# Attention and token/channel mixer on one core: 29 of 168 squares of score tiles moved to GpSimd

## The chip, the cores and the metric

The kernel runs on one core of one Trainium2 chip. The metric is device time in microseconds of one execution. A core has five engines with an in-order queue each: TensorE (PE in the profile; its weight loads, which run beside the matmuls, are PEld), VectorE (DVE), ScalarE (ACT), GpSimd (POOL) and SyncE (SP). Here GpSimd issues the input loads, and SyncE the transposing DMAs and the stores. Engines wait for each other by semaphores. Matmul results stand in PSUM, in eight banks, until VectorE or ScalarE has read them.

## The reference

Two parts, one behind the other (8 batches, 12 heads, 448 tokens, head size 64):

```python
scores = scale * np.matmul(q, k.transpose(0, 1, 3, 2))
attn = np.maximum(scores, 0.0) ** 2 / S
x = np.matmul(attn, v)                       # heads side by side: (8, 448, 768)
h = np.maximum(x.transpose(0, 2, 1) @ w_tok1, 0.0) @ w_tok2
u = x + h.transpose(0, 2, 1)
out = u + np.maximum(u @ w_ch1, 0.0) @ w_ch2
```

The attention has no softmax: a score is cut at zero and squared. The square is what the change is about. The factors `scale**2 / S` are applied later, when the product with `v` leaves PSUM.

## The kernel before

**Steps and pieces.** A step `s` is one third of a batch, four heads; there are 24 steps, three to a batch. Each step's scores fall into 7 pieces `c` of 64 keys. A piece `S{s}.{c}` is four matmuls of TensorE into two PSUM banks (line 515). Two evictions `r{s}.{c}.0` and `.1` cut it at zero and bring it to SBUF as bf16, on ScalarE (line 343) or on VectorE (line 345). One square `q{s}.{c}` then squares both halves in place, as one 128 x 896 tile of bf16, on ScalarE (`AF.Square`, line 355) or on VectorE (a product of the tile with itself, line 357). `V{s}.{c}`, four matmuls (line 542), multiplies the squared piece with `v`; the seven `V` of a step add up in two PSUM banks. The squared tiles live in a ring of 12 buffers inside the SBUF tile `arena`, so a piece's eviction waits for the `V` of the piece 12 before it. There are 24 x 7 = 168 squares.

**What follows a step.** The result leaves PSUM (`xe`, lines 552 and 554), is transposed, goes through the token mixer (`t1`, `rt`, `t2`, `u`, lines 588 to 601), and once a batch's three steps are there, through the channel mixer. The first two batches use plain products (`C1`, line 623); the others one level of Strassen's scheme: `M1` (line 780) with evictions `s1` and `d1` (793, 796), and `M2` (line 847) with evictions `d2` (860, 862). Strassen's sums and differences of operands (`w`, `tu`, `h`) are VectorE instructions that read two SBUF tiles (line 688).

**Loads.** Each step's k, q and v come by six loads `ldk`, `ldq`, `ldv` of 112 KB (line 371) on GpSimd's queue. From step 10 on, k and q are rearranged in SBUF (`ik`, `iq`, line 351 on VectorE or 349 on ScalarE) and transposed by DMA (`xk`, `xq`, line 497, on SyncE).

**What sets the order.** One table of words, `ORDER`, written out by hand or by a planner, is read from front to back: each word emits one operation, and so fixes its place on its engine's queue. `:A` and `:D` behind a word choose ScalarE or VectorE. Digits behind a PE word name the PSUM banks it takes: `C1.1.2:7` fills bank 7, `c1e1.2:D` empties it on VectorE, and `S8.1:37` takes banks 3 and 7 again, so that it waits for that eviction. A name behind a load (`ldv9.0:xd6`) holds the load back until the named DMA is done.

Of the kernel before, what the change touches and what calls it, by code (L numbers as in the profile page):

```python
# [10 lines left out]
ALU = mybir.AluOpType  # L11
# [26 lines left out]
class Order:  # L38
# [55 lines left out]
wc2.1 r4.0.1:D q4.6:A S4.3:63 C1.0.10:0 cp5.1:D r4.3.1:A cp5.0:D q4.5:D r4.1.1:A X3.0:7 r4.0.0:A q4.1:A  # L94
xc3.0:D C1.0.1a:5 C1.0.1 q4.0:D ldv5.0 c1e0.10:A t1.3.0:3 r4.3.0:D c1e0.1:A wc2.2 q4.4:A q4.3:D ldk7.0 S5.3:24
S5.1:17 V4.0:06 r5.1.0:A V4.1 r5.3.1:D V4.2 V4.3 rt3.0:A r5.3.0:D V4.4 V4.5 r5.1.1:A V4.6 S5.0:54 S5.6:12
xe4.1:D xe4.0:A T6.0:37 r5.6.1:A r5.0.0:D S5.2:06 r5.2.0:D cp6.0:A X4.0:2 r5.6.0:D C1.0.5:5 cp6.1:A ldv5.1
xc4.0:D r5.0.1:A r5.2.1:A S6.0:03 r6.0.1:D S5.5:17 S6.1:24 q5.1:A C1.0.6:6 ldq7.1 r6.1.1:D ldv6.1 q5.6:A
r5.5.0:D C1.0.7:3 ldq10.0 c1e0.5:D c1e0.6:A r6.0.0:D r6.1.0:A r5.5.1:D S6.3:41 S6.4:56 S5.4:02 q5.3:D
C1.0.0a:7 r6.3.0:A q5.2:A r6.3.1:A C1.0.8:4 r5.4.0:A r6.4.0:A ldv7.1 q5.0:D r5.4.1:A t2.3.0:1 r6.4.1:A q5.4:A  # L100
c1e0.8:D C1.0.9:0 u3.0:D c1e0.9:A q6.3:D t2.3.1:5 C1.0.0 ldq9.1 C1.0.11:4 u3.1:D q6.4:A c1e0.0:D t1.4.0:2
# [6 lines left out]
d2.0.0.11b:D ldk10.1:ub0.0 r7.4.1:D ldk9.0:ub0.1 t2.4.1:5 h0.0.3:D M2.0.0.6 h0.0.2:D d2.0.0.22a:D T8.0:32  # L108
S7.2:61 d2.0.0.12a:D r7.2.0:A M2.0.0.3 ldq9.0:ub0.1 w1.0.0:D q7.4:A ldq11.1 u5.0:D q6.0:A t2.4.0:6 w2.2.0:D
# [9 lines left out]
q8.6:D r9.0.1:A r9.0.0:D w1.1.0:D c1e1.10:D r9.4.1:A C1.1.3:5 xq11 q9.0:D q8.4:D t1.6.0:6 q9.4:A q8.5:A
t1.7.0:3 ldq13.0:st1.0 rt6.0:A iq12:D ub1.2 c1e1.6:A ldk12.1:st1.64 ldq13.1:xd7 c1e1.3:D S9.2:27 rt7.0:A  # L120
S9.3:41 q8.1:D q8.3:D V8.0:56 r9.2.0:D r9.3.0:A V8.1 V8.2 r9.2.1:D S9.1:03 r9.3.1:A V8.3 S9.5:24 r9.1.0:A
r9.1.1:D V8.4 ldk14.0:xk11 S10.1:71 V8.5 r9.5.1:A V8.6 S9.6:03 r9.5.0:D xe8.0:D ldk12.0 ldk15.1 r9.6.0:A
q9.2:A t2.7.0:4 q9.5:D ldk13.0:st1.0 r9.6.1:A C1.1.11:2 q9.1:D ldq15.1 q9.3:A C1.1.7:5 t2.6.0:0 ldk13.1:xq11
# [15 lines left out]
r12.6.0:A V11.5 w1.3.0:D r13.0.0:A S12.5:53 V11.6 xe11.1:A t2.9.0:0 st4.64 r12.5.0:D M1.2.0.1:1 ldv12.0:ub2.2
r12.5.1:A ldq16.0:xk14 u9.0:D r13.0.1:A M1.2.0.5:7 tu2.1:D r12.6.1:A iq14:D S12.4:53 xe11.0:A S12.1:02 q12.3:D  # L140
xd11 w1.3.2:D s1.2.0.1:A M1.2.2.5:4 M1.2.2.1:6 r12.4.1:A r12.4.0:A M1.2.0.2:3 ldk17.1:st4.0 w1.2.1:D
s1.2.0.5:A q12.6:D w1.3.1:D M1.2.0.6 ldq17.0:ub2.1 q12.4:A d1.2.0.11:D tu2.3:D ldk16.0:ub2.1 r12.1.0:D
ldv13.1:xk14 s1.2.2.1:A t2.9.1:5 q12.0:A M1.2.0.3 M1.2.4.1:3 u9.1:D ub3.1 M1.2.2.2:0 r12.1.1:A s1.2.0.2:A
M1.2.2.6 d1.2.2.11:D s1.2.2.2:A xq14 M1.2.0.7 d1.2.0.12:D s1.2.2.5:A q12.5:A q12.2:D d1.2.0.22:D t1.10.0:5
M1.2.2.3 rt10.0:A q12.1:D d1.2.2.12:D xq15 M1.2.0.4 q13.0:A M1.2.2.7 y1.2.0:D S13.3:20 d1.2.2.22:D S13.1:75
r13.1.1:D V12.0:41 V12.1 V12.2 r13.3.1:A st6.64 st3.64 r13.3.0:A V12.3 V12.4 st5.0 r13.1.0:A V12.5 V12.6
q13.3:D S13.5:05 ub2.3 S13.4:27 xe12.1:A r13.5.0:D M1.2.2.4 s1.2.4.1:A xe12.0:D r13.5.1:A M1.2.4.2:1 r13.4.1:D
# [17 lines left out]
q15.5:D r15.6.0:A ldv17.1:xd13 q15.6:D M1.3.0.4 ldk20.0:xd13 c2e1.6.1:D S16.3:75 q16.0:A V15.0:41 r16.3.1:A  # L165
V15.1 ik19:D r16.3.0:D V15.2 V15.3 y1.3.0:A S16.5:06 r16.5.1:D V15.4 S17.1:35 st13.64 r16.5.0:A ub3.4 V15.5
S16.6:72 V15.6 r17.1.0:A q16.1:D q16.3:D S17.3:06 r17.1.1:A M1.3.2.1:3 r16.6.1:A xq18 ik18:D M1.3.2.5:5
xe15.1:A xe15.0:D s1.3.2.1:A M1.3.2.2:2 r17.3.0:D xd15 M1.3.2.6 r16.6.0:A r17.3.1:A d1.3.2.11:D s1.3.2.5:A
S16.2:14 S16.4:07 s1.3.2.2:A S17.4:62 r17.4.1:A r16.4.1:D M1.3.2.3 xk18 r16.4.0:A t2.13.0:7 d1.3.2.12:D
q17.1:A iq19:A xk19 M1.3.2.7 st13.0 r16.2.0:D t1.14.0:2 d1.3.2.22:D st6.0 q16.5:D M1.3.4.1:0 ub4.0 s1.3.4.1:A  # L170
r17.4.0:A r16.2.1:D M1.3.4.2:5 q17.3:A q16.2:D M1.3.4.5:1 xq19 rt14.0:A d1.3.4.11:D M1.3.4.6 t2.13.1:4 st12.64
M1.3.2.4 s1.3.4.2:A u13.0:D t1.15.0:6 s1.3.4.5:A q16.4:D u13.1:D q16.6:A M1.3.4.3 q17.4:D ub4.2 y1.3.2:A
M1.3.4.7 ldq23.1:st13.0 d1.3.4.12:D S17.0:57 ldk23.0:st13.0 ik20:D d1.3.4.22:D V16.0:24 V16.1 r17.0.1:A
S17.2:31 ldv19.1:st13.0 r17.0.0:D V16.2 ldq20.0 t2.14.1:7 rt15.0:A M1.3.4.4 ldv18.1 u14.1:D r17.2.1:A S17.6:65
V16.3 r17.2.0:A ldq22.0 y1.3.4:A q17.2:D S17.5:17 V16.4 r17.6.0:D r17.5.0:D V16.5 r17.5.1:A S18.3:30 V16.6
t2.14.0:6 xe16.0:A M2.1.0.2:7 h1.0.0:D M2.1.0.5:1 r18.3.0:A ldv20.0 q17.5:D q17.0:A h1.0.2:D ldk21.0:st13.64
r17.6.1:A ldk21.1 u14.0:D xe16.1:A S18.0:23 V17.0:56 d2.1.0.11a:D r18.0.0:A r18.3.1:D V17.1 V17.2 V17.3
# [826 lines left out]
```

## Time and profile before

| | |
|---|---|
| median of 3 runs (lowest, highest) | 345.86 us (342.97, 346.24) |
| profiled execution: time, span of its instructions | 344.49 us, 342.7 us |
| PE busy | 333.9 us, 97% of the span |
| DVE busy | 294.7 us, 86% |
| ACT busy | 250.1 us, 73% |
| POOL busy (issuing loads, nearly all of it) | 92.1 us, 27% |
| squares on ACT, line 355 | 76, 72.3 us |
| squares on DVE, line 357 | 92, 55.1 us |
| granted TensorE clock | 1.00 |

Times of single instructions come from the one profiled execution. The ends of matmuls are modelled in it, so a PE that is shown busy may still be waiting for a moment between two matmuls. DVE and ACT instructions that follow each other overlap a little in the records, and "busy" counts such a stretch once.

### The profile page before, as it was taken

The numbers are of one execution on the slowest core, as the hardware profiler recorded it, in microseconds if no ns is written. First come the engines' busy times: TensorE is split into PE (matmuls) and PEld (weight loads), VectorE is DVE, ScalarE is ACT, GpSimd is POOL, SyncE is SP. The second block draws the span as 40 slices with busy tenths as digits, with TensorE's granted clock in tenths as the row PEclk, the third lists the DMA queues.
The fourth block names the chain that finished last, engine by engine and source line by source line (L and its number), as shares of the span: only waits on it lengthen the run. The fifth ranks groups of instructions, "written<-read, shape, count | busy, mean of one in ns | idle before, by whom it ended". The sixth has DMA issues, their size and how long they took to land.

```text
span 342.7 us, 9412 instructions
## 1 busy us (share of the span) xinstructions
PE 333.9 (97%) x3797; PEld 222.5 (65%) x3797; DVE 294.7 (86%) x571; ACT 250.1 (73%) x462; POOL 92.1 (27%) x157
## 2 busy tenths in 40 slices
PE   7899999999999999999999999999999999999995
PEld 4456665655565658865578555876578777887753
DVE  2999998899899999998998999789986986838783
ACT  4999999858899789989799898979785832221000
POOL 8985422624251343131240712020020000000000
PEclk9999999999999999999999999999999999999999
DMA  8999999999999999999999997997676113432255
GB/s 151 178 183 192 205 209 186 133 141 158 177 191 172 176 142 155 223 174 144 167 201 191 157 143 153 151 162 132 135 148 87 25 31 80 89 79 62 71 147 153
DMA packets 98940, 50.20 MB, mean 146 GB/s; under 512 B 71568, under 2 KB 95952, under 8 KB 98896
## 3 DMA queue, kind: packets, MB, share of 16 engines
q1 hardware_dynamic: 72736, 26.92, 46.4%
q0 software_dynamic: 25136, 21.47, 45.3%
q10 hardware_dynamic: 1024, 1.21, 1.2%
q8 instruction: 29, 0.48, 0.6%
q14 instruction: 15, 0.12, 0.2%
HBM read 43.38 MB, written 11.01 MB: 159 GB/s over the span
## 4 chain that ended last, share of the span: by engine, by line
PE 85%; DMA 5%; ACT 4%; DVE 3%; issue 1%; SPq 0%; POOL 0%; ACTq 0%; DVEq 0%
PE m_ps L780 20%; PE m_ps L847 20%; PE sc_ps L515 9%; PE acc_ps L542 8%; PE m_ps L623 8%; PE t_ps L588 6%; PE h_ps L597 5%; PE m_ps L713 4%; ACT arena L343 3%; DMA arena<-in_q_dram 3%; DMA x_sb<-xT 2%; PE kqT_ps L472 1%; PE warm_ps L414 1%; PE x_ps L579 1%; DVE uT L601 1%
## 5 line engine op out<-in xcount | busy, mean ns | idle before, releaser
L343 ACT ACTIVATE arena<-sc_ps 128x448 bf16<-128x448 f32 x232 | 117.1, 593 | 16.8 <-PE sc_ps L515 16.2
L355 ACT ACTIVATE arena<-arena 128x896 bf16<-128x896 bf16 x76 | 72.3, 969 | 0.4
L345 DVE TENSOR_SCALAR arena<-sc_ps 128x448 bf16<-128x448 f32 x104 | 62.0, 616 | 3.7 <-PE sc_ps L515 3.3
L515 PE MATMUL sc_ps<-arena 64*64 64x448 bf16 x672 | 54.9, 357 | 2.2 <-ACT arena L349 1.2
L357 DVE TENSOR_TENSOR arena<-arena 128x896 bf16<-128x896 bf16 x92 | 55.1, 615 | 1.1 <-ACT arena L343 0.5
L371 POOL DMA_DIRECT2D arena<-in_q_dram x46 | 28.4, 619 | 80.9 <-DMA arena<-arena 29.2
L780 PEld LDWEIGHTS <-wc 128*128 128x128 bf16 x432 | 40.9, 98 | 5.1 <-issue 2.3
L371 POOL DMA_DIRECT2D arena<-in_v_dram x48 | 29.5, 619 | 54.4 <-DMA out_dram<-out_sb 21.9
L542 PE MATMUL acc_ps<-arena 64*64 64x448 bf16 x672 | 43.1, 350 | 0.2
L515 PEld LDWEIGHTS <-arena 64*64 64x64 bf16 x672 | 22.3, 105 | 24.1 <-issue 15.6
L371 POOL DMA_DIRECT2D arena<-in_k_dram x48 | 29.9, 633 | 25.2 <-DMA out_dram<-out_sb 10.0
L780 PEld LDWEIGHTS <-ws 128*128 128x128 bf16 x324 | 30.8, 98 | 3.9 <-issue 1.7
L847 PE MATMUL m_ps<-wc,r 128*128 128x384 bf16 x162 | 30.3, 327 | 0.0
L601 DVE TENSOR_TENSOR uT<-h_ps,xT 128x448 bf16<-128x448 f32 x48 | 29.1, 616 | 1.2 <-PE h_ps L597 0.9
L847 PEld LDWEIGHTS <-r 128*128 128x128 bf16 x216 | 20.4, 98 | 14.8 <-issue 2.6
L623 PE MATMUL m_ps<-uT,wc 128*128 128x448 bf16 x144 | 29.9, 353 | 0.0
L542 PEld LDWEIGHTS <-arena 64*64 64x64 bf16 x672 | 20.9, 106 | 11.3 <-issue 3.1
L793 ACT ACTIVATE arena<-m_ps 128x448 f32<-128x448 f32 x18 | 9.2, 542 | 23.7 <-PE m_ps L780 8.3
L780 PE MATMUL m_ps<-uT,wc 128*128 128x224 bf16 x216 | 25.3, 259 | 0.0
L588 PE MATMUL t_ps<-x_sb,wt 128*128 128x256 bf16 (+1 forms) x216 | 25.0, 261 | 0.1
L597 PE MATMUL h_ps<-wt,r_sb 128*128 128x448 bf16 x96 | 25.1, 353 | 0.0
L847 PEld LDWEIGHTS <-sums 128*128 128x128 bf16 x180 | 17.2, 98 | 12.0 <-issue 1.0
(86 smaller groups left out, 510.5 us busy)
## 6 DMA issues: line engine op xcount, KB each, us to landing
out_dram<-out_sb SPq DMA_DIRECT2D x42, 192.0 KB, 3.3
arena<-in_k_dram POOLq DMA_DIRECT2D x48, 112.0 KB, 5.0
arena<-in_v_dram POOLq DMA_DIRECT2D x48, 112.0 KB, 5.3
arena<-in_q_dram POOLq DMA_DIRECT2D x46, 112.0 KB, 4.9
wc<-in_moe_w_ch_dram POOLq DMA_DIRECT2D x6, 768.0 KB, 13.1
out_dram<-arena SPq DMA_DIRECT2D x4, 192.0 KB, 2.7
out_dram<-out_sb SPq DMA_DIRECT2D x8, 96.0 KB, 2.1
out_dram<-out_sb ACTq DMA_DIRECT2D x8, 96.0 KB, 2.4
```

The costliest lines, as they stand in the source:

```text
L343: nc.scalar.activation(out, ps, AF.Relu)
L345: nc.vector.tensor_scalar(out=out, in0=ps, scalar1=0.0, scalar2=None, op0=ALU.max)
L355: nc.scalar.activation(x, x, AF.Square)
L357: nc.vector.tensor_tensor(out=x, in0=x, in1=x, op=ALU.mult)
L371: o.ins = nc.gpsimd.dma_start(out=raws[t][s % NR][64 * half:64 * (half + 1)], in_=src[b, h0:h0 + 2].rearrange('e (p c) d -> p e (c d)', c=KC))
L515: nc.tensor.matmul(o.ps[e][64 * half:64 * (half + 1), :S], lhsT=lhsT, rhs=rhs, start=True, stop=True, skip_group_check=True)
L542: nc.tensor.matmul(o.ps[half][64 * e:64 * (e + 1), :S], lhsT=r[rows, e, c * D:(c + 1) * D], rhs=sq[rows, e, :], start=c == 0, stop=c == KC ...
L588: nc.tensor.matmul(o.ps[:, j, :], lhsT=wt1[:, c, j * 128:(j + 1) * 128], rhs=x_sb[:, p0:p1, c, :], start=c == 0, stop=c == 3)
L597: nc.tensor.matmul(o.ps[:, :S], lhsT=r1[:, j, a * 128:(a + 1) * 128], rhs=wt2[:, j, :], start=j == 0, stop=j == JC - 1)
L623: nc.tensor.matmul(ps[:, :S], lhsT=wc1[:, g, e * 128:(e + 1) * 128], rhs=uT[:, g, off:off + S], start=g == 0, stop=g == CC - 1)
L780: nc.tensor.matmul(o.ps[:, j * HB:(j + 1) * HB], lhsT=lhs[:, g, (e + j) * 128:(e + j + 1) * 128], rhs=rhs[:, g], start=j == g == 0 and not ...
L847: nc.tensor.matmul(o.ps[:, :HN], lhsT=lhs[:, e], rhs=rhs[:, e], start=e == 0 and not on, stop=e == EC // 2 - 1, skip_group_check=True)
```

## The change

A third letter, `:P`, sends an operation to GpSimd, and `square` learns to emit a product of the tile with itself there. In `ORDER`, 29 squares of steps 4 to 20 carry that letter: 16 that stood on ScalarE and 13 that stood on VectorE. Their words also stand at other places, mostly earlier, beside loads on the same queue. TensorE's words, SyncE's words and the loads stand in the order in which they stood, and so do all other words of ScalarE and VectorE among themselves. The code below line 356 moves down by two lines, so GpSimd's squares are line 357 of the changed kernel and VectorE's line 359.

```diff
-            if how in ('A', 'D'):
-                o.on = 'ACT' if how == 'A' else 'DVE'
+            if how in ('A', 'D', 'P'):
+                o.on = {'A': 'ACT', 'D': 'DVE', 'P': 'POOL'}[how]
...
-wc2.1 r4.0.1:D q4.6:A S4.3:63 C1.0.10:0 cp5.1:D r4.3.1:A cp5.0:D q4.5:D r4.1.1:A X3.0:7 r4.0.0:A q4.1:A
+wc2.1 r4.0.1:D q4.6:A S4.3:63 q4.4:P C1.0.10:0 cp5.1:D r4.3.1:A cp5.0:D q4.5:D r4.1.1:A X3.0:7 r4.0.0:A q4.1:A
...
     def square(o, x):
         if o.on == 'ACT':
             nc.scalar.activation(x, x, AF.Square)
+        elif o.on == 'POOL':
+            nc.gpsimd.tensor_tensor(out=x, in0=x, in1=x, op=ALU.mult)
         else:
             nc.vector.tensor_tensor(out=x, in0=x, in1=x, op=ALU.mult)
```

On GpSimd's queue, around steps 8 and 9, before: the DMA rows are loads, the last names what each waits for (DMASW and DMAHW are landings of DMAs).

```order
L371 DMA arena<-in_k_dram 64x2x448 [waits DMAHW0_49,DMASW4_49,DVE_49]
L371 DMA arena<-in_q_dram 64x2x448 [waits DMASW5_49]
L371 DMA arena<-in_v_dram 64x2x448 [waits DMAHW6_49,DMASW6_49]
L371 DMA arena<-in_v_dram 64x2x448 [waits DMAHW3_49,DMASW7_49,PE_49]
L371 DMA arena<-in_q_dram 64x2x448 [waits DMAHW3_49,DMASW0_49,PE_49]
```

The same place after, with the squares `q8.2`, `q8.6`, `q8.4` and `q9.0` as TENSOR_TENSOR rows; each waits for the two evictions of its piece.

```order
L373 DMA arena<-in_k_dram 64x2x448 [waits DMAHW0_49,DMASW4_49,DVE_49]
L373 DMA arena<-in_q_dram 64x2x448 [waits DMASW5_49]
L357 TENSOR_TENSOR arena<-arena 128x896 [waits PE_49,Activation_49]
L357 TENSOR_TENSOR arena<-arena 128x896 [waits DVE_49,PE_49,Activation_49]
L357 TENSOR_TENSOR arena<-arena 128x896 [waits Activation_49]
L373 DMA arena<-in_v_dram 64x2x448 [waits DMAHW6_49,DMASW6_49]
L373 DMA arena<-in_v_dram 64x2x448 [waits DMAHW3_49,DMASW7_49]
L357 TENSOR_TENSOR arena<-arena 128x896 [waits DVE_49,PE_49,Activation_49]
L373 DMA arena<-in_q_dram 64x2x448 [waits DMAHW3_49,DMASW0_49,PE_49]
```

Three squares now stand in front of the loads `ldv9.0` and `ldv10.1`, and one behind them.

On VectorE's queue at that place, before: the rows of L357 are squares (`q8.2`, `q8.6`, then `q9.0` and `q8.4` as one row x2), those of L688 are Strassen sums of weights (`w1.1.1`, `w1.1.0`), and the rest are evictions.

```order
L345 TENSOR_SCALAR r_75<-m_ps 128x448
L357 TENSOR_TENSOR arena<-arena 128x896
L688 TENSOR_TENSOR ws<-ws,wc_67 128x768
L345 TENSOR_SCALAR arena<-sc_ps 128x448
L357 TENSOR_TENSOR arena<-arena 128x896
L345 TENSOR_SCALAR arena<-sc_ps 128x448
L688 TENSOR_TENSOR ws<-ws,wc_67 128x768
L345 TENSOR_SCALAR r_75<-m_ps 128x448
L357 TENSOR_TENSOR arena<-arena 128x896 x2
```

And after:

```order
L345 TENSOR_SCALAR r_75<-m_ps 128x448
L690 TENSOR_TENSOR ws<-ws,wc_67 128x768
L345 TENSOR_SCALAR arena<-sc_ps 128x448 x2
L690 TENSOR_TENSOR ws<-ws,wc_67 128x768
L345 TENSOR_SCALAR r_75<-m_ps 128x448
```

Four squares have left VectorE there; evictions and sums keep their order.

Further on, on GpSimd's queue after, five squares stand nearly together (`q16.0`, then `q16.3`, `q17.1`, `q17.3`, `q16.2`), where before the loads followed each other:

```order
L373 DMA arena<-in_v_dram 64x2x448 [waits DMASW5_49]
L357 TENSOR_TENSOR arena<-arena 128x896 [waits DVE_49,Activation_49]
L373 DMA arena<-in_k_dram 64x2x448 [waits DMASW6_49]
L357 TENSOR_TENSOR arena<-arena 128x896 [waits DVE_49,Activation_49]
L357 TENSOR_TENSOR arena<-arena 128x896 [waits Activation_49]
L357 TENSOR_TENSOR arena<-arena 128x896 [waits DVE_49,Activation_49]
L357 TENSOR_TENSOR arena<-arena 128x896 [waits DVE_49]
L373 DMA arena<-in_q_dram 64x2x448 [waits DMAHW0_49,DMASW7_49,Activation_49]
```

The load of k for step 20 (`ldk20.0`) stands behind the first of the five, and `ldq23.1` behind the last.

More of the change, by code (lines that the diff above doesn't have):

```diff
@@ L119 @@
[L119 to L123, printed above, removed]
@@ L139 @@
[L139 to L143, printed above, removed]
@@ L144 @@
[L144 to L147, printed above, removed]
+w1.0.2:D r8.2.1:A q7.1:D q7.6:A xk10 S8.3:61 iq11:D q8.2:P S8.6:35 q7.5:D c1e1.1:D V7.0:04 V7.1 r8.3.1:A
@@ new lines @@
+ldv12.1:ub2.2 ik14:D t2.8.1:2 d2.0.5.22b:D ldk16.1:xk13 ldv13.0 S12.0:67 q11.5:A u8.1:D S12.2:40 rt9.0:A
+M2.0.5.3 tu2.2:D ub2.5 r12.2.1:A r12.2.0:D r12.0.0:A M2.0.5.4 r12.0.1:A q12.2:P xk14 q11.2:A q11.6:D S12.3:23
+S12.6:04 d2.0.5.21:D V11.0:67 V11.1 r12.3.0:A d2.0.5.12b:D V11.2 V11.3 xd10 r12.3.1:A iq15:D V11.4 S13.0:12
+tu2.0:D r12.6.0:A V11.5 q12.3:P w1.3.0:D r13.0.0:A S12.5:53 V11.6 xe11.1:A t2.9.0:0 st4.64 r12.5.0:D
+M1.2.0.1:1 ldv12.0:ub2.2 r12.5.1:A ldq16.0:xk14 u9.0:D r13.0.1:A M1.2.0.5:7 tu2.1:D r12.6.1:A iq14:D S12.4:53
@@ L164 @@
 t1.13.0:0 ldv18.0 d1.3.0.12:D q15.3:A C2.1.6.1:3 ldv17.0:xq16 d1.3.0.22:D r16.1.0:A r16.0.1:D rt13.0:A st11.64
[L165 to L177, printed above, removed]
-r18.0.1:A ldk22.0:ub4.0 q17.6:D S19.1:47 ldq21.0:xq19 S19.0:02 V17.4 V17.5 r19.1.0:D ldk22.1 V17.6 M2.1.0.1:3
```

208 lines of the change are left out of this document (115 added, 93 removed).

## The prediction

> **What bounds the kernel now.** I read the page first, then the stages, then TensorE's own waits. The page gives the busy time by engine and, at the end, the engines on the chain of waits that ended last.
>
> ```profile
> span 342.7 us, 9412 instructions
> PE 333.9 (97%) x3797; PEld 222.5 (65%) x3797; DVE 294.7 (86%) x571; ACT 250.1 (73%) x462; POOL 92.1 (27%) x157
> ...
> PE 85%; DMA 5%; ACT 4%; DVE 3%; issue 1%; SPq 0%; POOL 0%; ACTq 0%; DVEq 0%
> ```
>
> The changed squares stand between about 40 and 222 us, so I cut the span at 40 and 240. The columns are PE, PEld, DVE, ACT and POOL busy, then the granted clock, the DMA share and GB/s.
>
> ```profile
> 40.00:240.00 200.00, 199.12 (x2294) 128.36 (x2287) 184.84 (x357) 177.49 (x322) 59.40 (x100) 1.00 1.16 168
> 240.00:320.00 80.00, 79.57 (x740) 61.32 (x739) 61.41 (x118) 38.00 (x70) 2.36 (x4) 1.00 0.40 79
> 320.00:342.70 22.70, 18.51 (x130) 11.91 (x128) 14.99 (x31) 0.00 (x0) 0.00 (x0) 1.00 0.52 139
> ```
>
> TensorE is idle for 200 - 199.12 = 0.88 us in the stage of the change, and 0.43 us in the next. All its waits from 40 to 320 us are these:
>
> ```profile
> PE sc_ps L515 <- DVE uT L601: 0.5, 1, 0.5
> PE m_ps L780 <- ACT arena L793: 0.4, 1, 0.4
> PE sc_ps L515 <- DVE out_sb L722: 0.2, 1, 0.2
> ```
>
> So TensorE is the bound at full granted clock, and the whole gain that relief of other engines can give is 0.88 + 0.43 = 1.3 us; the idle 4.2 us at the end, after the last matmuls, belong to evictions and stores that the change does not touch. The other side is open. VectorE is busy 184.84 of 200 us beside it and ScalarE 177.49. How little room there is between an eviction and the matmul that takes the bank again shows in the order of time; the first row reads bank 7 (`c1e1.2`), the second fills it again (`S8.1`).
>
> ```profile
> 87.26 0.61 DVE L345 TENSOR_SCALAR r<-m_ps 128x448 bf16<-128x448 f32 x1
> ...
> 87.97 0.48 PE L515 MATMUL sc_ps<-arena 64*64 64x448 bf16 x4
> ```
>
> The eviction ends at 87.87, the matmul starts at 87.97: 0.1 us. There a VectorE that is 1 us late costs TensorE 0.9 us.
>
> **The change part by part.** What goes: 13 squares from VectorE and 16 from ScalarE, by these rows of the stage from 40 to 240 us.
>
> ```profile
> L357 DVE TENSOR_TENSOR arena<-arena 128x896 bf16<-128x896 bf16 x57 | 34.6, 616 | 1.0 <-ACT arena L343 0.5
> L355 ACT ACTIVATE arena<-arena 128x896 bf16<-128x896 bf16 x62 | 58.7, 966 | 0.3
> ```
>
> VectorE loses 13 x 0.616 = 8.0 us, ScalarE 16 x 0.966 = 15.5 us. Neither ends a wait of TensorE of any size, so by itself this is worth between 0 and -1.3 us; I take 0, because each of the three waits came once and ended with an eviction, none with a square.
>
> What comes: 29 squares on GpSimd. The trace has no such instruction. The nearest rows are GpSimd's own in the setup.
>
> ```profile
> masks.py:199 POOL TENSOR_SCALAR_AFFINE_SELECT ident<-ident 128x128 bf16<-128x128 bf16 x1 | 0.3, 288 | 0.1
> masks.py:197 POOL MEMSET ident<- 128x128 bf16 x1 | 0.2, 231 | 0.0
> L988 POOL MEMSET const-bfloat16-1.0<- 128x1 bf16 x1 | 0.1, 102 | 0.0
> ```
>
> One column costs 0.10 us, which is the fixed part. The select reads one operand and takes (0.288 - 0.10) / 128 = 1.47 ns a column more, so 896 columns with one operand would be 0.10 + 1.32 = 1.4 us. The square has two operands; read one after the other they would be 0.10 + 2.64 = 2.7 us. I take 2.1 us, halfway, and keep both ends. [...]
>
> The squares themselves can be hidden. GpSimd is busy 59.4 of the 200 us; 29 x 2.1 = 61 us more leaves it at 60%. What is queued behind a waiting or running square are loads. The tightest squares are the five around 175 to 187 us, of which `q16.2` is the last.
>
> ```profile
> 174.66 0.60 POOL L371 DMA_DIRECT2D arena<-in_v_dram  x1 [0.40 <-DMA arena<-in_k_dram]
> ...
> 175.30 0.72 POOL L371 DMA_DIRECT2D arena<-in_k_dram  x1
> ...
> 175.51 0.38 DVE L351 COPY arena<-arena 128x896 bf16<-128x896 bf16 x1
> ```
>
> ```profile
> 189.25 0.36 PE L542 MATMUL acc_ps<-arena 64*64 64x448 bf16 x4
> ```
>
> The first of the five can start at 175.3, behind `ldv17.0`; one load of 0.7 us stands between, so the fifth ends at 176.0 + 5 x 2.1 = 186.5, and `V16.2`, the matmuls that need it, start at 189.25: 2.7 us to spare. The cover is gone above (189.25 - 176.0) / 5 = 2.65 us a square. Of the loads, the closest is `ldv12.0`, which now waits for `q12.2` and `q12.3`.
>
> ```profile
> 126.38 1.24 POOL L371 DMA_DIRECT2D arena<-in_v_dram  x2
> ```
>
> ```profile
> 140.37 0.55 PE L542 MATMUL acc_ps<-arena 64*64 64x448 bf16 x8
> ```
>
> The row of these loads among the DMA issues of that stretch ends with the time to landing.
>
> ```profile
> arena<-in_v_dram POOLq DMA_DIRECT2D x2, 112.0 KB, 6.3
> ```
>
> It was the second of the two at 126.38 (about 127.0). Behind two squares it is issued at 127.0 + 4.2 = 131.2, lands 6.3 us later at 137.5, and `V12.0` needs it at 140.37: hidden, with 2.9 us left. So as long as nothing else is disturbed, the squares and loads cost 0.
>
> What may be disturbed is VectorE. A product of two SBUF operands on GpSimd runs beside VectorE's own: the squares that stay (57 - 13 = 44) and the Strassen sums of line 688, whose row in the same stage is
>
> ```profile
> 40.00:240.00 200.00, 34.13 (x63) 1.00 1.16 168
> ```
>
> That makes 44 + 63 = 107 VectorE instructions with two SBUF operands in 200 us, 0.535 per us. Nothing in the trace says what happens when one meets a GpSimd square, so I bound it. Least: both run at full speed, 0. Most: the two engines cannot read SBUF for two operands at once, and VectorE's instruction waits, with all behind it, until the square is done. For a square of 2.1 us the chance that one falls due is 1 - exp(-0.535 x 2.1) = 0.675, and the mean wait 2.1 - 0.675 / 0.535 = 0.84 us; 29 squares make 24.3 us (12.0 at 1.4 us a square, 36.9 at 2.7). The rows around 90 us show how thick they stand; first the last load in front of `q8.2` on GpSimd and the eviction of ScalarE for which `q8.4` waits, then VectorE.
>
> ```profile
> 85.97 0.62 POOL L371 DMA_DIRECT2D arena<-in_q_dram  x1
> ```
>
> ```profile
> 90.06 0.62 ACT L343 ACTIVATE arena<-sc_ps 128x448 bf16<-128x448 f32 x1
> ```
>
> ```profile
> 90.28 0.61 DVE L357 TENSOR_TENSOR arena<-arena 128x896 bf16<-128x896 bf16 x1
> 90.81 0.55 DVE L688 TENSOR_TENSOR ws<-ws,wc 128x768 bf16<-128x768 bf16 x1
> 91.64 0.62 DVE L345 TENSOR_SCALAR arena<-sc_ps 128x448 bf16<-128x448 f32 x1 [0.28 <-PE sc_ps L515]
> 92.19 0.62 DVE L357 TENSOR_TENSOR arena<-arena 128x896 bf16<-128x896 bf16 x1
> 92.72 0.62 DVE L345 TENSOR_SCALAR arena<-sc_ps 128x448 bf16<-128x448 f32 x1
> 93.25 0.55 DVE L688 TENSOR_TENSOR ws<-ws,wc 128x768 bf16<-128x768 bf16 x1
> ```
>
> With 2.1 us each, `q8.2`, `q8.6` and `q8.4` run one after another on GpSimd from 86.6 (85.97 + 0.62) to 92.9, the third from 90.8, just after its eviction is done (90.68). The sum of line 688 at 90.81 falls on the seam between two of them; the two evictions behind it (91.64, 92.72) free score banks that TensorE waits for. What of the 24.3 us reaches the end: 8.0 are paid by the squares that left VectorE; of its idle time, 200 - 184.84 = 15.2 us, between none and all can be used. That is 24.3 - 8.0 - 15.2 = 1 us at the least and 16 at the most. By the margin of 0.1 us above it is nearer to none, but a stall of TensorE also gives VectorE its lead back; I take half the idle time, 7.6: 24.3 - 8.0 - 7.6 = 8.7 us.
>
> Load issuing does not disturb VectorE in this way: the 57 squares on VectorE average 616 ns in the stage in which GpSimd issued about a hundred loads. A faint sign for a shared path is the load at 175.30, 0.72 us against 0.60 of the one before it, which ran over a VectorE copy between two SBUF tiles (175.51, above). [...]
>
> **The sum.** Against the profiled execution: 344.49 + 0 (relief) + 0 (squares and loads hidden) + 8.7 (VectorE held) = 353.2 us. That execution lies inside the runs of before (342.97 to 346.24, median 345.86), 1.8 us above its span.
>
> **The rivals.** (1) Nothing is held: the squares vanish behind TensorE. For it: TensorE idles 0.4% of the stage, and every cost above has cover. Against it: it needs 107 VectorE instructions to pass 29 squares freely. Time 344.5, from 343.2 (all idle of TensorE gone) to 346.5. It decides if the wait per square is below about (8.0 + 7.6) / 29 = 0.54 us. (2) GpSimd itself becomes late: a square over 2.65 us. At 3.5 us the five squares end at 193.5, 4.3 us behind `V16.2`, and `ldv12.0` lands at 127.0 + 7.0 + 6.3 = 140.3, just in time: 344.5 + 4.3 = 348.8. Against it: 3.5 lies above the upper end of 2.7. (3) Faster by over 1%: it would need 3.5 us where TensorE idles 1.3; only a change in how densely TensorE's matmuls follow each other, which the page models, could give it: 341 us. That the squares do not move at all is out: they stand on GpSimd's queue in the rows above.
>
> **How the numbers follow.** VectorE held 0.60, nothing held 0.33, GpSimd late 0.04, faster 0.03. The trace alone leaves the hold open between none and full; I lean to it because TensorE's slack lets through no gain and any hold beyond 0.54 us a square, out of a possible 0.84, costs time. The likeliest case by itself runs from 345.5 (24.3 us with all idle used) to 361 (none used, 16.3 more); with a square of 2.7 us it goes to 344.5 + 36.9 - 8.0 - 7.6 = 365.8, with 1.4 us to 344.5. About 1% is what a measurement of this kernel can tell from no change, that is 3.5 us. Of the 0.60, 0.55 are over it; with 0.04 of GpSimd late and 0.01 of the rest: slower 0.60. Same: 0.05 + 0.31 = 0.36. Faster 0.04. The range takes in nothing held and the full hold at 2.1 us, and leaves out some 0.05 below 343.5 and 0.12 above 361.
>
> **What would show it.** In the changed profile: the squares' row on GpSimd at 2.1 us (1.4 to 2.7); if they are held or hold, VectorE's rows for its own squares (line 359) and sums (line 690) rise above 616 and 550 ns, or gaps stand before them, VectorE's busy or waiting time in the stage goes up by some 16 us net though 13 squares left, and TensorE gets waits for VectorE's evictions of several us where it had 0.7. If those rows stay at their length and TensorE's waits stay near 1 us, the hold is wrong and the time is that of rival 1. Matmuls `V16.2` or `V12.0` waiting for GpSimd or a load would show rival 2. The prediction is wrong in its main step if a square takes 2 us and VectorE's two-operand rows are unchanged.

## The result

The changed kernel takes 358.24 us (median of 4 runs, 356.01 to 360.61) against 344.49 us before (median of 4, 342.97 to 346.24): a ratio of 1.0391, with a 95% interval of 1.0331 to 1.0451. It is 13.75 us slower. Its four executions fall into two pairs, 356.01 and 356.32 us at a mean granted clock of 1.00, 360.16 and 360.61 us at 0.993 and 0.995, and the profiled one is the longest, with a span of 357.3 us.

The page of the changed kernel, its span, the busy time by engine, and the engines on the chain that ended last:

```profile
span 357.3 us, 9449 instructions
PE 339.7 (95%) x3797; PEld 223.7 (63%) x3797; DVE 305.4 (85%) x558; ACT 237.8 (67%) x446; POOL 142.4 (40%) x186
...
PE 71%; DVE 12%; issue 5%; DMA 5%; POOL 3%; ACT 2%; DVEq 0%; ACTq 0%; POOLq 0%
```

VectorE has 13 instructions fewer and is busy 10.7 us longer (294.7 before); TensorE's share of the chain falls from 85 to 71% and VectorE's rises from 3 to 12%. The stages show where the time went. The stage of the change holds the same matmuls (2294 before, 2292 now) when it is cut at 254 us instead of 240; the columns are those of the prediction's rows.

```profile
40.00:254.00 214.00, 204.29 (x2292) 129.25 (x2291) 195.46 (x344) 165.05 (x306) 110.56 (x130) 0.99 1.05 157
254.00:334.00 80.00, 79.57 (x739) 61.20 (x737) 61.42 (x117) 38.58 (x71) 2.36 (x4) 1.00 0.41 79
334.00:357.30 23.30, 19.10 (x135) 12.39 (x132) 15.57 (x31) 0.00 (x0) 0.00 (x0) 1.00 0.51 136
```

Of the 14.6 us by which the span is longer, 14.0 lie in the first row: 214 us where it was 200. TensorE's idle time there is 214 - 204.29 = 9.71 us (0.88 before), and its busy time for the same matmuls is 5.2 us more; about 1.7 of these go with a lower clock (below), and the rest is not traced to a cause. The next stage is the same as before, the last 0.6 us longer. What TensorE waits for, of all that the kernel shows from 0.9 us up (who waits, for whom, us in total, times, longest):

```profile
PE sc_ps L517 <- DVE xT L556: 4.1, 2, 3.1
PE m_ps L849 <- DVE out_sb L864: 1.9, 3, 1.3
PE sc_ps L517 <- ACT arena L349: 1.2, 2, 0.7
PE warm_ps L416 <- DVE out_sb L413: 1.2, 1, 1.2
PE m_ps L849 <- DVE out_sb L862: 1.2, 1, 1.2
PE sc_ps L517 <- DVE out_sb L724: 0.9, 2, 0.7
PE sc_ps L517 <- DVE arena L345: 0.9, 3, 0.5
```

The first two and the fifth and seventh are evictions by VectorE that were not among the waits before, and the sixth has grown from 0.2; the other two were there with the same 1.2. The five make 9.0 us. None of the new ones is for a square, and for a load TensorE waits 0.2 us. So VectorE is late with its evictions. The groups of the stage from 40 to 254 us say why. First GpSimd's squares, from the page, then VectorE by form of instruction (count, busy us, mean ns of one):

```profile
L357 POOL TENSOR_TENSOR arena<-arena 128x896 bf16<-128x896 bf16 x29 | 49.8, 1721 | 43.3 <-ACT arena L343 21.4
```

```profile
L345 DVE TENSOR_SCALAR arena<-sc_ps 128x448 bf16<-128x448 f32 x79 | 47.0, 615 | 3.0 <-PE sc_ps L517 2.9
L359 DVE TENSOR_TENSOR arena<-arena 128x896 bf16<-128x896 bf16 x44 | 31.3, 717 | 0.6 <-ACT arena L343 0.2
...
L351 DVE COPY arena<-arena 128x896 bf16<-128x896 bf16 x19 | 12.4, 652 | 1.0 <-issue 1.0
...
L690 DVE TENSOR_TENSOR r<-r 128x768 bf16<-128x768 bf16 x7 | 5.3, 761 | 0.0
...
L690 DVE TENSOR_TENSOR ws<-wc,ws 128x768 bf16<-128x768 bf16 x3 | 3.1, 1040 | 0.0
```

The same forms before, from 40 to 240 us (the row of the squares, 616 ns, stands in the prediction):

```profile
L345 DVE TENSOR_SCALAR arena<-sc_ps 128x448 bf16<-128x448 f32 x79 | 47.2, 616 | 2.1 <-PE sc_ps L515 2.0
...
L351 DVE COPY arena<-arena 128x896 bf16<-128x896 bf16 x19 | 7.4, 387 | 1.7 <-DMA arena<-in_q_dram 1.5 <-issue 0.2
...
L688 DVE TENSOR_TENSOR r<-r 128x768 bf16<-128x768 bf16 x7 | 3.8, 549 | 0.0
...
L688 DVE TENSOR_TENSOR ws<-wc,ws 128x768 bf16<-128x768 bf16 x3 | 1.6, 549 | 0.0
```

The evictions, which read PSUM, are as long as before (615 ns against 616). The instructions that read and write only SBUF are longer: the squares 717 against 616, the sums up to 1040 against 549, and the copies, which the prediction had not counted, 652 against 387. Taken one by one (the duration of each VectorE instruction behind 30 us, less the median of its form before, counted where it is over 60 ns), 17 instructions are longer, 18.0 us in all. Five of them are copies, 5.1 us. The others all have two SBUF operands, and none reads PSUM. Where one ends behind a GpSimd square, it does so at a nearly constant distance: 0.48 us for a square of VectorE, 0.36 to 0.42 for a sum, 0.25 for a copy. That is the look of an instruction that is on record as started, stands until the square is done, and runs then.

The largest is a copy at 108.69 us: VectorE first, then GpSimd's queue, where `q10.1` and `q10.4` run one right behind the other.

```profile
107.09 0.61 DVE L603 TENSOR_TENSOR uT<-h_ps,xT 128x448 bf16<-128x448 f32 x1
108.69 3.06 DVE L351 COPY arena<-arena 128x896 bf16<-128x896 bf16 x1 [0.99 <-issue]
111.68 0.54 DVE L690 TENSOR_TENSOR sums<-r 128x768 bf16<-128x768 bf16 x1
112.15 0.61 DVE L556 TENSOR_SCALAR xT<-acc_ps 128x448 bf16<-128x448 f32 x1
```

```profile
107.56 0.59 POOL L373 DMA_DIRECT2D arena<-in_k_dram  x1 [0.61 <-PE sc_ps L517]
108.17 3.33 POOL L357 TENSOR_TENSOR arena<-arena 128x896 bf16<-128x896 bf16 x2
```

The copy (`ik12`) first comes 0.99 us late, because it waits for a load whose last packet lands at 108.62, and is then held for 2.68 us more than its 0.38; the pair of squares ends at 111.50, the copy 0.25 behind it. The eviction of line 556 stands in the queue two places further back, and it is the 3.1 us wait of TensorE in the table above. What followed was not in the prediction; in 2 us pieces, the granted clock is the third number from the end:

```profile
108.00:110.00 2.00, 1.71 (x15) 0.64 (x12) 1.30 (x1) 2.00 (x5) 1.99 (x3) 1.00 1.35 105
110.00:112.00 2.00, 0.00 (x0) 0.00 (x0) 2.00 (x2) 0.62 (x2) 1.50 (x1) 1.00 1.34 180
112.00:114.00 2.00, 1.19 (x8) 0.40 (x8) 2.00 (x5) 0.04 (x1) 0.00 (x0) 0.61 1.32 239
114.00:116.00 2.00, 2.00 (x8) 0.94 (x7) 1.82 (x4) 2.00 (x4) 0.64 (x1) 0.53 1.12 227
```

After standing for 3.1 us TensorE ran at 0.61 and 0.53 of its clock for 4 us, about 2 x 0.39 + 2 x 0.47 = 1.7 us more. The mean clock of 1.00 in 356.01 and 356.32 leaves no room for this fall; whether the stall was in them is not known, since only one execution was profiled.

### The profile page after: what moved, and what is told of

The parts are those of the page before. It is cut to its first block, busy times and chain, and to the rows that moved or that the text cites. A ratio compares the mean times of both kernels' runs of the same rounds, so it can differ in the third digit from the quotient of the medians.

```text
span 357.3 us, 9449 instructions
## 1 busy us (share of the span) xinstructions
PE 339.7 (95%) x3797; PEld 223.7 (63%) x3797; DVE 305.4 (85%) x558; ACT 237.8 (67%) x446; POOL 142.4 (40%) x186
## 4 chain that ended last, share of the span: by engine, by line
PE 71%; DVE 12%; issue 5%; DMA 5%; POOL 3%; ACT 2%; DVEq 0%; ACTq 0%; POOLq 0%
PE m_ps L849 19%; PE m_ps L782 18%; PE sc_ps L517 8%; PE m_ps L625 7%; PE acc_ps L544 7%; PE t_ps L590 5%; PE h_ps L599 4%; PE m_ps L715 3%; DMA arena<-in_q_dram 2%; POOL arena L373 2%; DMA arena<-arena 2%; DVE arena L359 2%; DVE arena L345 2%; DVE sums L690 2%; DVE out_sb L864 1%
## 5 line engine op out<-in xcount | busy, mean ns | idle before, releaser
L357 POOL TENSOR_TENSOR arena<-arena 128x896 bf16<-128x896 bf16 x29 | 49.8, 1721 | 43.3 <-ACT arena L343 21.4
L517 PE MATMUL sc_ps<-arena 64*64 64x448 bf16 x672 | 58.0, 360 | 7.8 <-DVE xT L556 4.1
L355 ACT ACTIVATE arena<-arena 128x896 bf16<-128x896 bf16 x60 | 57.3, 968 | 1.9 <-DVE arena L345 1.7
L359 DVE TENSOR_TENSOR arena<-arena 128x896 bf16<-128x896 bf16 x79 | 51.9, 672 | 0.7 <-ACT arena L343 0.2
L517 PEld LDWEIGHTS <-arena 64*64 64x64 bf16 x672 | 22.9, 105 | 32.9 <-issue 24.6
L849 PE MATMUL m_ps<-wc,r 128*128 128x384 bf16 x162 | 31.3, 334 | 0.0
L544 PEld LDWEIGHTS <-arena 64*64 64x64 bf16 x672 | 21.4, 106 | 11.1 <-issue 3.5
L798 DVE CUSTOM_DVE_ANT_0 r<-r,m_ps 128x448 bf16<-128x448 f32 x32 | 19.6, 615 | 6.6 <-PE m_ps L782 4.3
```

Of the source, the lines that this page charges most:

```text
L355: nc.scalar.activation(x, x, AF.Square)
L357: nc.gpsimd.tensor_tensor(out=x, in0=x, in1=x, op=ALU.mult)
L359: nc.vector.tensor_tensor(out=x, in0=x, in1=x, op=ALU.mult)
L517: nc.tensor.matmul(o.ps[e][64 * half:64 * (half + 1), :S], lhsT=lhsT, rhs=rhs, start=True, stop=True, skip_group_check=True)
L544: nc.tensor.matmul(o.ps[half][64 * e:64 * (e + 1), :S], lhsT=r[rows, e, c * D:(c + 1) * D], rhs=sq[rows, e, :], start=c == 0, stop=c == KC ...
L849: nc.tensor.matmul(o.ps[:, :HN], lhsT=lhs[:, e], rhs=rhs[:, e], start=e == 0 and not on, stop=e == EC // 2 - 1, skip_group_check=True)
```

## The experiments

The theory from these rows: a GpSimd instruction that reads SBUF holds VectorE's SBUF instructions, and with them the evictions behind them. The rivals: GpSimd's extra work costs in some other way (its queue, its loads, its semaphores); each square costs about the same wherever it stands; ScalarE and VectorE were worth more than TensorE's idle time showed. Each ratio below is against executions of the kernel before from the same session, whose medians run from 344.37 to 345.95 us; so the ratios compare better than the times.

**e1: the work of GpSimd alone.** All squares back on ScalarE and VectorE, and at the 29 places on GpSimd's queue two idle products on a tile that nothing else uses (the second waits for the first, since it reads what that wrote).

```diff
-            q4.4:P   (and 28 more)
+            g4.4     (and 28 more, squares as in the kernel before)
+                for _ in range(2):
+                    o.ins = nc.gpsimd.tensor_tensor(out=idle, in0=idle, in1=idle, op=ALU.mult)
```

> All 168 squares are back on ScalarE and VectorE as before; at the 29 places of GpSimd's queue stand instead two products each of an idle 128x448 tile with itself (about 1.7 us together), which wait for the same evictions as the square did and whose result nobody uses. Theory hold (a GpSimd product that reads SBUF keeps VectorE's two-operand instructions and SBUF copies waiting until it ends): VectorE's rows for squares and sums lengthen as in the changed kernel, and nothing is relieved, so as slow or slower than the changed kernel: 356 to 368 us. Theory queue (the squares cost because loads behind them on GpSimd come late): the same time as with idle writes instead of products, no longer VectorE rows. If what cost time was that a V matmul waited for a square on GpSimd: 344 to 346.

**e2: the same places, memsets.** Three idle memsets in place of the two products.

```diff
-                for _ in range(2):
-                    o.ins = nc.gpsimd.tensor_tensor(out=idle, in0=idle, in1=idle, op=ALU.mult)
+                for _ in range(3):
+                    o.ins = nc.gpsimd.memset(idle, 0.0)
```

> As the run with idle products, but three idle writes of a 128x448 tile (no operand read, about 1.7 us together) in place of each pair of products. Theory hold through the read path: two-operand rows of VectorE keep 616 and 550 ns; at most its copies between SBUF tiles are held; 344 to 348 us. If any GpSimd work beside VectorE holds it, or if the loads behind it are what is late: the same time as with the products.

e1 took 353.57 us, a ratio of 1.0261 (1.0203 to 1.0319); e2 344.79 us, 0.9995 (0.9961 to 1.0028). GpSimd's group of each:

```profile
L533 POOL TENSOR_TENSOR idle<-idle 128x448 bf16<-128x448 bf16 x58 | 60.2, 1037 | 42.0 <-ACT arena L344 23.5 <-DVE arena L346 12.8 <-DVE arena L352 2.8
```

```profile
L533 POOL MEMSET idle<- 128x448 bf16 x87 | 41.5, 477 | 41.3 <-ACT arena L344 25.2 <-DVE arena L346 12.4
```

So 60 us of products that nobody waits for cost 9 us, and 41 us of memsets in the same places cost nothing that can be measured. The products read SBUF and the memsets do not, and both stand in the same queue behind the same waits; so the queue and the waits are not the cause. (That the memsets are shorter is not it either: e8 below has 80 us in these places and loses 1%.) That it is the reads and not the arithmetic no run shows by itself; with one operand less to read the loss is smaller (e8). In e1 30 VectorE instructions are longer, 14.5 us in all, five of them copies; in e2 two copies, 0.4 us, each beside a memset. e1 lost less than expected, since none of its instructions is held for more than 0.77 us: VectorE gets its turn in the 0.08 us between two products. Here two of its squares and a copy pass, one behind each of the first three of four products in a row:

```profile
183.21 2.40 DVE L358 TENSOR_TENSOR arena<-arena 128x896 bf16<-128x896 bf16 x2
185.54 1.12 DVE L352 COPY arena<-arena 128x896 bf16<-128x896 bf16 x1
```

```profile
182.93 4.51 POOL L533 TENSOR_TENSOR idle<-idle 128x448 bf16<-128x448 bf16 x4 [0.37 <-DVE arena L346]
```

e2's profiled execution, 349.17 us, shows a late load and not a hold: `ik12` waits 2.49 us for it there (0.99 in the changed kernel, none in e1), and TensorE then stands for 1.99 us. So at this place a late load alone stalls TensorE, too.

**e3 and e4: the 29 squares in two parts.** e3 moves only the 12 squares that met no lengthened VectorE instruction in the changed kernel's trace, e4 only the other 17.

```diff
 e3: :P only on q4.4 q5.3 q5.6 q6.3 q8.2 q8.6 q8.4 q9.0 q12.1 q13.3 q17.3 q18.2
 e4: :P only on q7.4 q10.1 q10.4 q10.2 q11.1 q12.2 q12.3 q15.1 q15.2 q16.0 q16.3
                q17.1 q16.2 q19.1 q19.2 q19.4 q20.2
```

> Only the 12 squares during which no VectorE instruction was longer in the changed kernel's trace are on GpSimd (q4.4 q5.3 q5.6 q6.3 q8.2 q8.6 q8.4 q9.0 q12.1 q13.3 q17.3 q18.2); the other 17 are back where they were. Theory hold: the time of before, 343 to 347 us, as far as no new meeting comes up. If every square on GpSimd costs its share: 344.5 + 12/29 x 13.8 = 350 us.

> Only the other 17 squares are on GpSimd, those that overlapped a lengthened VectorE instruction. Theory hold: nearly the whole loss, 354 to 360 us. If every square costs its share: 344.5 + 17/29 x 13.8 = 352.6 us.

e3 took 346.24 us, 1.0047 (1.0015 to 1.0079), e4 354.45 us, 1.0287 (1.023 to 1.0344). Twelve squares cost 1.9 us and seventeen 10.1; by an even share it would have been 5.7 and 8.1. e3 speaks against the even share; e4 alone would not, with 2 us between its result and that share. In e4 17 instructions are longer, 15.5 us; in e3 two, 0.4 us. The two losses add up to 12.0 of the 13.75 us; the long hold of the copy by `q10.1` and `q10.4` in a row, and the clock after it, do not show in e4, although it has the pair as well. What the 1.9 us of e3 are is not settled: in its profiled execution (348.77 us, its longest) a load that landed late shows, and hardly a hold.

**e5: the pair taken apart.** `q10.1` and `q10.4` back on ScalarE, the other 27 as changed.

```diff
-q10.1:P ... q10.4:P
+q10.1:A ... q10.4:A
```

> The change with the two squares q10.1 and q10.4 given back to ScalarE, 27 squares left on GpSimd. In the changed kernel these two ran back to back, the copy ik12 on VectorE was recorded 3.06 us long behind them, and TensorE then stood for about 3 us and ran at a granted clock of 0.53 to 0.61 for the 4 us after. Hold (VectorE stands while a GpSimd square runs, and what counts is how long one instruction is held at a time): the stall of TensorE between 107 and 112 us is gone, the other sixteen held instructions stay; 350 to 354 us, so 4 to 8 us come back for 2 of 29 squares. Rival, every square costs about the same (13.75 us / 29 = 0.47 us each): 357.3 us. Rival, the clock drop and a late load make the stall, not the hold: 357 to 359 us and the stall at 107 to 112 us still there.

356.29 us, 1.0331 (1.0275 to 1.0386). The stall at 107 to 112 us is gone, as expected of the hold: the copy is short again, and no 2 us piece of the profile has a granted clock under 0.97.

```profile
107.91 0.39 DVE L351 COPY arena<-arena 128x896 bf16<-128x896 bf16 x1
```

But not 4 us came back; by the ratios it is 0.006 of 344.5, about 2, with intervals that overlap. The time by itself (354.0 to 357.8 us by its interval) fits the even share of 357.3 better than the 350 to 354 of the hold; it is the trace that speaks for the hold. Two reasons show for the small gain. 356.29 is what the two executions of the change at full clock took (356.01 and 356.32), so the costly stall may have been in the two others only. And the rest of the order met GpSimd elsewhere. Ten us later stands `q10.2`, which in the changed kernel held a sum for 0.99 us. Here it holds another one for 2.10 us, and that one was started 0.49 us ahead of it, while GpSimd still issued a load:

```profile
117.52 2.65 DVE L690 TENSOR_TENSOR sums<-sums,r 128x768 bf16<-128x768 bf16 x1
```

```profile
117.41 0.64 POOL L373 DMA_DIRECT2D arena<-in_q_dram  x1
118.01 1.74 POOL L357 TENSOR_TENSOR arena<-arena 128x896 bf16<-128x896 bf16 x1
```

So the size was a miss: which instruction meets a square is decided by a few tenths of a microsecond, and a stall taken out at one place can move the meetings behind it.

**e6 and e11: the squares in halves.** e6 makes each square two products of 448 columns; e11 puts a memset between the halves.

```diff
-            nc.gpsimd.tensor_tensor(out=x, in0=x, in1=x, op=ALU.mult)
+            for e in range(2):
+                nc.gpsimd.tensor_tensor(out=x[:, e], in0=x[:, e], in1=x[:, e], op=ALU.mult)
 e11, between the two:
+            nc.gpsimd.memset(idle, 0.0)
```

> Each of the 29 squares on GpSimd as two products of 128x448 with no wait between them, in place of one of 128x896. Hold lasting for one GpSimd instruction, and VectorE let in between two of them: a held instruction waits at most about 0.9 us in place of up to 1.7 us, its wait is about half as long, and the time falls to 348 to 353 us. If the next GpSimd instruction takes hold before VectorE gets in: as the change, 356 to 360 us. Rival, the cost is GpSimd's own time: the halves take a little longer together than one whole (two times the 0.89 us seen for bare 128x448 products against 1.68 us), so 358 to 361 us.

> The change with each of the 29 squares as two products of 128x448 and, unlike e6, an idle memset of 128x224 on GpSimd between them (the memsets of e2 hardly held VectorE). If it lets VectorE in between the halves: no VectorE instruction is held over two products (three were in e6, by 1.7 to 2.4 us), none longer than about 0.95 us, and 349 to 352 us. If it does not: as e6, 353 to 356 us. GpSimd's square is longer, about 2.2 us; one is due within 3.16 us of its operand (q16.2), so rival: where GpSimd comes late, TensorE waits for GpSimd at the V matmuls (L544) and 355 us or more.

e6 took 353.66 us, 1.0212 (1.013 to 1.0293), e11 355.75 us, 1.0293 (1.0205 to 1.0382). e6 lies just above its first expectation (inside it by the ratio, 351.8), e11 in the second of its own. The halves brought part of the loss back; with the memset less of it, if any. (A product of 128x448 takes 0.93 us by itself in e1 and e6, not the 0.89 of the expectation.) In e6 most holds end with one half, yet three last over more; in e11 one lasts over three halves and the memset between the first two:

```profile
86.75 3.90 DVE L361 TENSOR_TENSOR arena<-arena 128x896 bf16<-128x896 bf16 x1
```

```profile
86.58 0.62 POOL L375 DMA_DIRECT2D arena<-in_q_dram  x1
87.19 0.98 POOL L357 TENSOR_TENSOR arena<-arena 128x448 bf16<-128x448 bf16 x1
88.06 0.32 POOL L358 MEMSET idle<- 128x224 bf16 x1
88.31 0.97 POOL L359 TENSOR_TENSOR arena<-arena 128x448 bf16<-128x448 bf16 x1
89.19 0.96 POOL L357 TENSOR_TENSOR arena<-arena 128x448 bf16<-128x448 bf16 x1
90.07 0.31 POOL L358 MEMSET idle<- 128x224 bf16 x1
```

Each of these GpSimd records begins before the one ahead of it has ended (88.06 against 88.17), where in e1 0.08 us lie between. VectorE's square ended at 90.65, 0.50 us behind the third half, and TensorE waited for it at the V matmuls:

```profile
PE acc_ps L548 <- DVE arena L361: 2.3, 1, 2.3
```

That is a square of VectorE, not of GpSimd: the rival of a late GpSimd does not show, though a square took about 2.1 us there (the 3.16 us of the expectation are what `q16.2` had to spare behind its end in the changed kernel). So with a wait between two of GpSimd's products VectorE got in each time (longest hold 0.77 us in e1, and 0.63 in e10 below); where they follow at once, it gets in at some seams and not at others, memset or not. What decides it there is open.

**e7: the squares left out.** No engine computes the 29 squares.

```diff
+        if f'q{s}.{c}' in LEFT_OUT:
+            sq_ops[s, c] = ev
+            return u
```

> The 29 squares are left out altogether: they run on no engine, so ScalarE is rid of 16 and VectorE of 13 instructions and GpSimd has none. This gives the most that the relief could be worth. TensorE bounds the kernel and stands idle for 1.3 us between 40 and 320 us: 343 to 345 us, ratio 0.996 to 1.000. Rival, the two engines set a part of the pace by ways that the trace of before does not show as idle time of TensorE (a granted clock, say): 338 to 342 us, and then the holds cost that much more than the 13.75 us by which the change is slower.

343.97 us, 0.9987 (0.995 to 1.0025). Free removal of 23.5 us of work from the two engines is worth nothing that can be measured; TensorE is the bound, and with the rest of the order as it is, no other place for these squares can be expected to gain more.

**e9: relief and hold together.** The idle products of e1, and the 29 squares left out as in e7.

> The idle products of e1 at the same 29 places (two of 128x448 each), and the 29 squares left out altogether, as in e7. So GpSimd does what it did in e1, while VectorE is rid of 13 squares of 0.616 us (8.0 us) and ScalarE of 16 of 0.966 us (15.5 us). It tells whether relief of VectorE covers its holds, as the prediction's sum had it. e1 lost 9.2 us with 14.8 us held. If relief covers hold: 9.2 - 8.0 = 1.2 us are left, 345 to 347 us. If a hold costs where it strikes and relief elsewhere in the table gives nothing back: 351 to 354 us, as e1, with 25 or more VectorE instructions lengthened by 13 us or more.

350.95 us, 1.0131 (1.0066 to 1.0196), between the two expectations. Against e1 that is 0.013 of 344.5, 4.5 us (1.5 to 7.5 by the two intervals, which do not overlap). 25 instructions are longer, 11.7 us (14.5 in e1, by the count used here; the expectation has 14.8): part of what the relief gave is that fewer instructions stood there to be held. So 8.0 us taken from VectorE (with 15.5 from ScalarE) are worth roughly half of the 8.0 where holds set the pace, and zero where they don't (e7).

**e8 and e10: the kind and the length of GpSimd's instruction.** Both are e1 with another idle instruction.

```diff
 e8:
-                    nc.gpsimd.tensor_tensor(out=idle, in0=idle, in1=idle, op=ALU.mult)
+                    nc.gpsimd.tensor_scalar(out=idle, in0=idle, scalar1=0.0, scalar2=None, op0=ALU.max)
 e10, tensor_tensor on a tile of 224 columns:
-                for _ in range(2):
+                for _ in range(4):
```

> As e1 (all squares on ScalarE and VectorE, idle GpSimd work put beside them at the 29 places), but each idle product of two operands is replaced with an idle tensor_scalar maximum of one operand and the same 128x448 tile. If GpSimd holds VectorE only while it reads two operands from SBUF, as little as the memsets of e2: 344 to 346 us. If any read from SBUF holds it: as e1 in proportion to the time of one, 350 to 355 us with 15 or more VectorE instructions lengthened.

> As e1 (all squares on ScalarE and VectorE, idle products on GpSimd at the 29 places), but four products of 128x224 in place of two of 128x448, each again waiting for the one before. The sum of GpSimd's work is about the same (some 60 us) and the single hold is halved, to 0.45 us at most. If a queue in front of TensorE swallows some 0.2 to 0.3 us of each hold and only what is above it counts: 346 to 349 us. If the sum of the held time counts whatever its pieces (e1: 9.2 us for 14.8 held, 0.62): as many held us, more instructions, 351 to 354 us.

```profile
L533 POOL TENSOR_SCALAR idle<-idle 128x448 bf16<-128x448 bf16 x58 | 80.4, 1386 | 27.1 <-ACT arena L344 14.5
```

```profile
L533 POOL TENSOR_TENSOR idle<-idle 128x224 bf16<-128x224 bf16 x116 | 77.0, 664 | 26.8 <-ACT arena L344 12.7 <-DVE arena L346 3.9 <-DVE arena L352 2.5
```

e8 took 347.91 us, 1.0101 (1.0069 to 1.0133): with more time on GpSimd than e1, 22 instructions are longer by only 5.8 us, and most end while GpSimd's instruction still runs. Neither expectation was right: a one-operand read does disturb VectorE, but not until its end. e10 took 349.97 us, 1.0145 (1.0061 to 1.0229), again between its two: 34 instructions are longer, 10.3 us, the longest by 0.63 and not 0.45. The shorter pieces cut the sum of the holds (14.5 in e1); whether they also pass on a smaller share of it cannot be told, since the interval of e10 allows 2 to 8 us.

All of them side by side (held: VectorE instructions longer than before, counted as above in the profiled execution, which in e2, e3, e7 and e9 took 2.5 to 4.5 us more than the median):

| run | GpSimd work added, us | held | held, us | longest, us | time, us | ratio |
|---|---|---|---|---|---|---|
| the change | 49.9 | 17 | 18.0 | 2.68 | 358.24 | 1.0391 |
| e5 without the pair | 46.6 | 15 | 16.3 | 2.10 | 356.29 | 1.0331 |
| e11 halves, memset between | 65.9 | 26 | 17.0 | 3.28 | 355.75 | 1.0293 |
| e4 the 17 | 29.6 | 17 | 15.5 | 1.49 | 354.45 | 1.0287 |
| e1 idle products | 60.2 | 30 | 14.5 | 0.77 | 353.57 | 1.0261 |
| e6 halves | 58.4 | 21 | 17.3 | 2.42 | 353.66 | 1.0212 |
| e10 idle quarters | 77.0 | 34 | 10.3 | 0.63 | 349.97 | 1.0145 |
| e9 idle products, no squares | 57.4 | 25 | 11.7 | 0.77 | 350.95 | 1.0131 |
| e8 idle one-operand | 80.4 | 22 | 5.8 | 0.68 | 347.91 | 1.0101 |
| e3 the 12 | 20.5 | 2 | 0.4 | 0.35 | 346.24 | 1.0047 |
| e2 idle memsets | 41.5 | 2 | 0.4 | 0.26 | 344.79 | 0.9995 |
| e7 squares left out | 0 | 0 | 0 | 0 | 343.97 | 0.9987 |

The time does not follow GpSimd's work (29.6 us of it cost 2.9%, 80.4 cost 1.0%). It goes with the time that VectorE was held: in the runs with more than 5 us of it, the loss by the ratio is about 40 to 75% of the held time. The order is not strict (e6 has more held time than e4 and the smaller loss, though their intervals overlap), and the profiled execution need not be the typical one.

## Why the prediction was right, and where its sum was not

The direction, the mechanism and the place were right, and 358.24 lies in the range; the predicted 353.2 was 5.0 us too low, and that it came so near is in part luck. Step by step:

- **TensorE is the bound, relief is worth 0.** Right: e7 shows 0.9987 for the relief by itself.
- **A square on GpSimd takes 2.1 us.** Too long. It took 1.72 on the mean, from 1.67 to 2.05, inside the bounds of 1.4 and 2.7.
- **The squares and loads are hidden.** Right for the squares: by the records each was done at least 3.16 us (`q16.2`) before its V matmuls began, and no such wait appears. For loads it is not quite right: the copy at 108.69 waited 0.99 us for one, and that put it beside the pair of squares that held it.
- **VectorE is held for 24.3 us.** Held, yes; 18.0 us. With 1.72 us a square the prediction's own formula gives 1 - exp(-0.535 x 1.72) = 0.60 and a mean of 1.72 - 0.60 / 0.535 = 0.60 us, 17.3 us for 29 squares. The closeness is luck in part: the formula counts only instructions with two SBUF operands, and these were held for 18.0 - 5.1 = 12.9 us; the copies, which it leaves out, made up the rest. With the 19 copies counted in (126 in 200 us, 0.63 per us) it gives 0.67 us a square and 19.4 us. So its form was good, and the duration and the copies were the misses.
- **8.0 us of that are paid by the relief and 7.6 by half of VectorE's idle time.** This is the term that failed. Of 18.0 us only 18.0 - 13.75 = 4.3 were paid by the median, 18.0 - 14.6 = 3.4 by the span of the execution in which they were counted, not 15.6. e9 against e1 puts the relief at about 4.5 us instead of 8.0, which leaves nothing for the idle time in the change; yet e1, without relief, passes on 9 of its 14.5 us, so there is some cover where the holds are short. The prediction had the reason in hand: an eviction ended 0.1 us before TensorE needed its bank. The reading that fits is that a hold costs where it strikes, and that idle time of VectorE at other places of the stage does little against it; no run separates the two payments inside the change.
- **The sum.** The two wrong terms offset each other. With the true duration the prediction's sum would have been 344.5 + 17.3 - 15.6 = 346.2, and further off than it was.
- **Not foreseen:** the clock that falls after a stall of 3 us (1.7 us in the profiled execution), and two squares in a row (3.3 us) acting as one hold.

Of the signs that it named, TensorE's waits of several microseconds for VectorE, the longer rows of lines 359 and 690, and a busier VectorE all came, the last with 10.7 us (18.0 - 8.0 = 10.0) where 16 were named. Rival 1 (nothing held) falls with e1 beside e2. Rival 2 (GpSimd late) has no wait of TensorE for GpSimd in any of the traces. Rival 3 (faster) falls with e7.

## What to carry to other kernels

Before giving work to an idle engine, ask what else it shares with the busy ones: in these runs GpSimd products that read SBUF stopped VectorE's SBUF-to-SBUF instructions (17 of them for 18.0 us in the change and 30 for 14.5 us in e1, against two for 0.4 us beside the memsets of e2), and everything in VectorE's queue behind them (TensorE stood 3.1 us for the eviction at 112.15), even where no semaphore joins the two. Count such meetings near their full price (about 40 to 75% came through here) unless the place itself has slack, since idle time and relief elsewhere paid little for a wait in front of the bound engine (4.3 of 18.0 us in the change, by the median). And when the engine that bounds the kernel hardly idles (0.88 of 200 us here), first measure what leaving the work out altogether would bring (here nothing) before looking for a cheaper place for it.

## What the runs showed of the hardware

- **A hold looks like a long instruction, not like a gap.** The held instruction is on record as started, mostly with no idle time in front, and ends 0.25 to 0.5 us after the GpSimd product. Read the mean duration of a group against the kernel before.
- **GpSimd is held as well.** Of the 29 squares of the change, 21 took 1.67 to 1.70 us. The other eight, 1.71 to 2.05 us, all began while a VectorE instruction between SBUF tiles was running (of the 21, two did, in its last 0.04 us, and the second square of the pair at 108.17 began while the copy stood); the longest, at 188.83, began while a square of VectorE that the one before it had held ran until 189.34.
- **The hold can begin before the product.** In e5 and e11 VectorE instructions that were started 0.4 to 0.5 us ahead of a product, while GpSimd was still issuing a load, did not get done until products had ended (117.52 and 86.75 above). In the changed kernel a copy at 87.31, with the issue of two loads and no product beside it, was 0.10 us longer than its 0.38, though the prediction had read from the squares' rows that issuing disturbs nothing. Whether it is the issue that takes hold there was not tried.
- **One operand or two.** In e8 VectorE instructions were longer by 0.1 to 0.4 us mostly (22 of them, 5.8 us in all), and often ended inside the GpSimd instruction: the square at 56.66 took 0.97 us and ended at 57.63, GpSimd's one-operand pair at 57.92. Beside the two-operand products of the change 16 of the 17 ended 0.24 to 0.48 us after the product; the other, the copy at 87.31, had none beside it.
- **The clock after a stall.** In the 13 profiled executions TensorE stood longer than 1.6 us in one piece six times: 3.10 (the change), 2.69 (e7), 2.26 (e11), 2.25 (e9), 1.99 (e2) and 1.67 us (e3). After five of these (all but the 1.99) some of the next 4 to 6 us ran at a granted clock of 0.50 to 0.53. After stalls of 1.4 us and less it never did.
